# Later free times for five buffers, and three own banks for the whole of the last product

## The chip, the cores and the metric

The kernel runs on one core of a Trainium2 chip. The metric is the device time of one execution in microseconds (us). "DVE" is the vector engine, "ACT" the scalar engine, "PE" the tensor engine, "PEld" its weight loads, and "SP" the engine whose queue issues nearly all DMAs.

## The reference, cut to what matters

```python
# q, k, v: (8, 12, 448, 64); w_in: (768, 2048), w_out: (2048, 768); s, b: scalars
scores = q @ k.T / sqrt(64) - log(448)          # per batch and head
x = (sigmoid(scores) @ v)                       # regrouped to 3584 tokens x 768
h = x @ w_in
g = s * max(h, 0)**2 + b
out = g @ w_out                                 # 3584 x 768
```

## The kernel before, in words

Products in full precision are made of three reduced ones: every operand is split into a high and a low part (`PARTS`), and hi*hi, hi*lo and lo*hi are added up in PSUM. Weights arrive as 64-bit floats and are turned into 32-bit ones on chip (`convert`).

The program has three stretches. Each of the three engines and SP works in the order in which its instructions were emitted.

**Attention.** 24 steps, each with four heads of one batch (`quads`). A step ends with `store_x`: two copies from PSUM into an `xo` buffer on DVE and one DMA of 448 KB to DRAM. There are two `xo` buffers, used in turn.

**The first 512 tokens ("plain").** 16 slices of the hidden dimension, in the list `order` (0, 8, 1, 9, ...). For each slice PE makes `ffn1` (18 matmuls into a bank `ph`), ACT and DVE make the activation (relu, square, scale and bias, high part, low part: `activate`), and two slices later PE makes `ffn2` (18 matmuls). `ph` has two banks, so a slice's `ffn1` also waits for the relu of the slice two before. The weights of a slice are split by the class `Part`: high part on ACT (line 694), low part on DVE (line 638), then a store. Besides, DVE and ACT make sums of weight blocks for what comes later (`row_sums`), which nothing in this stretch needs.

**The other 3072 tokens.** Two groups of three tiles of 512 tokens. The two matrix products of each tile triple are done by a scheme with fewer products than the plain one: sums of blocks of the operands are multiplied (29 products a layer, each in two halves p = 0 and 1 of 12 matmuls of 512 columns), and results are sums of products (`sums`, `accs`). Products are chained in PSUM: a chain adds each new product onto the bank of the last one, so that the bank holds a running sum. Each of the lists `seq` has pairs (product, lane), and a lane is one PSUM tile of two banks, tagged b0 to b3. The last layer's list ends with (3, 0), (9, 1), (15, 0), (19, 1), (20, 0). The chain of lane 0 is 4, 3, 15, 20.

The order of all instructions of the last two stretches is made by a planner on the host (`Flow.run`). It has a cost for each operation, PE's order is given, and at each step it emits the operation that can start first, and of several the one due first. Where an operation needs a buffer, it can't start before the planned time at which a buffer is free (`heap.ready`). A buffer is taken from the front of a list that is sorted by that time (`Slots.tile`). The planner's time zero is the start of the plain stretch, where `ffn1` of slice 0 starts; DVE is planned from 2.0 on.

The set of buffers `cx` has 8 of its own, and from the plain stretch on 5 more, `t0` to `t4` (6 KB a partition each, in the pool `t2`). These 5 lie where the attention's buffers were: in the order in which the pools are laid out, `t0` overlaps the second `xo` buffer by 1 KB, from which the last step (the 24th) stores. At the start of the plain stretch 5 of the 8 own buffers are held: four by the tokens (`x0`), one by the weights `w1` of slice 0, which is freed by `ffn1(0)`. Two loads of weights (`convert_late`, on SP) and all weight parts of the first layer are put in `cx` as well. The second layer's parts lie in three buffers of their own, `p2`.

The very last half product (product 20, p = 1) is written differently (`last`): not onto the bank of lane 0, but in three pieces into banks of three other tags: 512 columns of the first half of the rows, and the second half in two pieces of 256 columns. The result block is then `part` (all other terms, joined on DVE with the bank of lane 0, which by then holds 4, 3, 15 and the first half of 20) plus the three pieces (`last_out`, three operations on DVE, each followed by its store).

Of the kernel before, what the change touches and what calls it, by code (L numbers as in the profile page):

```python
# [11 lines left out]
F32 = mybir.dt.float32  # L12
# [24 lines left out]
TB = 512  # L37
# [76 lines left out]
        seq=((20, 1), (23, 0), (14, 1), (27, 0), (5, 1), (18, 0), (25, 1), (13, 0), (0, 1), (17, 0),  # L114
         (15, 1), (28, 0), (3, 1), (21, 0), (19, 1), (1, 0), (24, 1), (26, 0), (22, 1), (10, 0),
         (16, 1), (11, 0), (4, 1), (7, 0), (2, 1), (9, 0), (12, 1), (8, 0), (6, 1)),
# [60 lines left out]
        seq=((0, 0), (2, 1), (1, 2), (17, 3), (27, 0), (28, 1), (21, 2), (22, 3), (18, 0), (10, 1),  # L177
         (6, 2), (13, 3), (5, 0), (26, 1), (11, 2), (12, 3), (25, 0), (23, 1), (8, 2), (16, 3),
         (4, 0), (24, 1), (7, 2), (14, 3), (3, 0), (9, 1), (15, 0), (19, 1), (20, 0)),
# [250 lines left out]
def build(net, layers, n_groups, raw_at, keep):  # L430

    flow, em = net.flow, net.em
    last = {}
    for n in range(n_groups):
        blocks = {}
        for l, L in enumerate(layers):
            seq, fresh = L["seq"], {c[0] for c in L["chains"]}
            np_ = L["np"]
            opds = {}
            count = {}  # L440
            for r, _ in seq:
                count[L["operand"][r][1:]] = count.get(L["operand"][r][1:], 0) + 1
            if l == 0:
                raw = {k: raw_at(n, k) for k in L["blocks"]}
                gets = [net.sums(raw, L["sums"], f"a{n}")] * np_
                ends = [
                    {k: (lambda v, s, k=k, p=p: blocks.__setitem__((k, p), keep(n, k, p, v, s))) for k in L["out"]}
                    for p in range(np_)
                ]
                have = [net.gather(L["accs"], ends[p], f"G{n}{p}") for p in range(np_)]  # L450
            else:
                gets = [
                    net.sums({k: blocks[em.home(k, p)] for k in L["blocks"]}, L["sums"], f"g{n}{p}")
                    for p in range(np_)
                ]
                accs = L["accs"]
                final = {k: (lambda v, s, k=k: em.out(net, n, k, v)) for k in L["out"]}
                end = n + 1 == n_groups
                if end:
                    r_last = seq[-1][0]  # L460
                    (k_last,) = (k for k, t in accs.items() if f"S{r_last}" in dict(t))
                    s_last = dict(accs[k_last])[f"S{r_last}"]
                    accs = {k: tuple(x for x in t if x[0] != f"S{r_last}") for k, t in accs.items()}
                    rest = []
                    final[k_last] = lambda v, s: rest.append((v, s))
                have = [net.gather(accs, final, f"C{n}", True)]
            for x, (r, lane) in enumerate(seq):
                row, name, sign = L["operand"][r]
                for p in range(np_):
                    key = (name, sign, p if l else 0)  # L470
                    if key not in opds:
                        v = gets[p](name)
                        opds[key] = net.split(v, sign, f"{'sg'[l]}{n}_{r}_{p}")
                        opds[key].uses = count[name, sign] * (1 if l else np_)
                    o = opds[key]
                    tag = 2 * lane + p if l == 0 else lane
                    new = r in fresh and (l == 0 or p == 0)
                    if l == 0 or p == 0:
                        bank = Bank(tag, l, None if new else last[tag])
                        waits = last[tag].readers if tag in last else []  # L480
                        last[tag] = bank
                    else:
                        bank, waits = last[tag], []
                    stop = l == 0 or p == np_ - 1
                    final_unit = l and end and x == len(seq) - 1 and p == np_ - 1
                    if final_unit:
                        part = net.join(*rest[0], Val(u, 1, bank), s_last, f"C{n}_e", True)
                        part.name = k_last
                        waits = [q for t, b in last.items() if t != tag for q in b.readers]

                    ended = None
                    seeds = r in L["seeds"] and not (l and end and x == len(seq) - 1)
                    if seeds and (l == 0 or p == 0):
                        seed = net.seeded(have[p if l == 0 else 0], f"S{r}", bank, waits, f"e{n}{l}_{r}_{p}")
                    if seeds and seed:
                        if l == 0 or p == 0:
                            waits = [seed[2]]
                        new = False
                        ended = seed

                    def fn(n=n, l=l, r=r, p=p, o=o, bank=bank, new=new, stop=stop, final_unit=final_unit):
                        if final_unit:
                            em.last(n, r, p, o, bank.tag)
                        else:
                            em.unit(n, l, r, p, o, bank, new, stop)
                        o.uses -= 1
                        if not o.uses:
                            flow.heap.free(o.hi)
                            flow.heap.free(o.lo)

                    u = em.matmuls(flow, net.UNIT, fn, [o.by, *waits], n, l, r, p)
                    if final_unit:
                        flow.op("DVE", 2.0, lambda: em.last_out(n, part, s_last), (u, part.by))
                    if stop and ended:
                        v = Val(u, 1, bank)
                        if l == 0:
                            ends[p][ended[0]](v, ended[1])
                        else:
                            final[ended[0]](net.copied(v, ended[1], f"C{n}_{ended[0]}"), 1)
                    elif stop and not final_unit:  # L520
                        have[p if l == 0 else 0](f"S{r}", Val(u, 1, bank))
# [3 lines left out]
def sigmoid_attention_relu2_ffn(  # L525
# [11 lines left out]
    B, NQ, P, _, _, S = qk.shape  # L537
    D = v.shape[5]
    NF, _, DM = w_in.shape
# [13 lines left out]
    def pool(stack, name, bufs, side=None, space=None):  # L553
        kw = dict(side=side) if side else {}
        if space is not None:
            kw["space"] = space
        return stack.enter_context(
            tc.tile_pool(name=name, bufs=bufs, reuse_waits="tile", **kw)
        )
# [37 lines left out]
    cx = Slots(cx_pool, 8, "c", spare=3)  # L597
# [24 lines left out]
    def paired(ap):  # L622
        return ap.rearrange("p (a b) -> p b a", a=2)
# [388 lines left out]
    for n, (b, t) in enumerate(quads):  # L1012
# [27 lines left out]
        last = al if n else firsts[0]  # L1040
        if n + 1 < NL:
            al = scores_last(*quads[n + 1], loaded[n + 1])
        attn_v_last(loaded[n], last, pav)
        if n and n + 1 in TWO:
            parts_lo(loaded[n + 1])
# [12 lines left out]
    rt, p2, gp = Slots(rt_pool, 2, "r"), Slots(p2_pool, 3, "w"), Slots(gp_pool, 3, "g")  # L1058
    ps_o = pool(blk_ps, "ps_o", 1, space=PSUM)
    t2 = pool(blk, "t2", 1)  # L1060
    cx.more(t2, 5, "t")
    wfp_late = pool(blk, "wfp_late", 1)
    for _, f in late:
        wf_tile(0, f, wfp_late)
# [29 lines left out]
    LAST = ((0, slice(0, TB)), (1, slice(0, TB // 2)), (1, slice(TB // 2, TB)))  # L1094

    class Emit:
# [74 lines left out]
                        )  # L1171
                        m += 1

        def last(self, n, r, p, o, busy):
            wt = fetched[stream.index((n, 1, r, p))]
            tags = [x for x in range(4) if x != busy]
            self.ends = []
            for e, tk in LAST:
                b = ps.tile([P, 2, TB], F32, tag=f"b{tags.pop(0)}", name=f"o_{e}_{tk.start}")[:, 0, tk]
                q = 0  # L1180
                for f in range(2):
                    for wi, gi in PARTS:
                        nc.tensor.matmul(
                            b, wt[:, f, wi, e * P : (e + 1) * P], paired((o.hi, o.lo)[gi][:, f, tk]),
                            start=q == 0, stop=q == 5, skip_group_check=True,
                        )
                        q += 1
                self.ends.append(b)

        def last_out(self, n, part, sign):  # L1190
            m, k = self.block[part.name]
# [51 lines left out]
    em = Emit()  # L1243
    net = Net(flow, em)
# [360 lines left out]
    plain()  # L1605
    later_sums(*LATER_SUMS)
    build(net, LAYERS, len(threes), load_raw, finish)
    flow.run({"DVE": 2.0})

# [38 lines left out]
```

## Time and profile before

| | |
|---|---|
| median of 3 runs | 977.67 us (976.95 to 978.43) |
| the profiled execution, its own time | 977.93 us |
| its span, first to last instruction | 976.1 us |
| PE busy | 970.9 us, 5192 matmuls |
| PE weight loads busy | 764.8 us |
| DVE busy | 875.8 us, 995 instructions |
| ACT busy | 719.8 us, 807 instructions |
| granted TensorE clock | 1.0 of full speed in every slice |

The span is what the profiler saw between the first and the last instruction; the device time holds 1.8 us more. A busy PE is not PE at its best, since the ends of matmuls are modelled and overlap; the distance between starts is the better measure.

### The profile page before, as it was taken

To read this page: it belongs to the slowest core of one execution; us is meant where nothing else is said; L and a number is where in the kernel's file an instruction comes from. 1 tells how busy PE (TensorE), PEld (TensorE's weight loads), DVE (VectorE), ACT (ScalarE), POOL (GpSimd) and SP (SyncE) were. 2 spreads that over 40 slices of the span, in tenths; PEclk is the share of its full clock that TensorE was granted. 3 is DMA by queue.
4 is the path that set the end of the run, shared out by engine and by line. 5 is a ranking of instruction groups with operands and counts; after the bars stand their busy time and mean duration, and the time that the engine had idled before them with its cause. 6 is when DMAs were issued, how large, how long until landed. Compare 5 with 4: busy or idle time off the path is not lost.

```text
span 976.1 us, 13892 instructions
## 1 busy us (share of the span) xinstructions
PE 970.9 (99%) x5192; PEld 764.8 (78%) x5192; DVE 875.8 (90%) x995; ACT 719.8 (74%) x807; POOL 0.2 (0%) x4
## 2 busy tenths in 40 slices
PE   9999999999999999999999999999999999999998
PEld 4555545555788888888888888888888888888887
DVE  5998999999899988899999999999787649999995
ACT  7999999999777767557799996333457499995330
POOL 0000000000000000000000000000000000000000
PEclk9999999999999999999999999999999999999999
DMA  8789999998569999989986666799866666666675
GB/s 327 286 308 350 326 364 401 351 396 311 191 263 365 354 403 413 414 279 320 341 287 206 202 203 205 226 333 330 311 201 202 207 200 207 200 205 202 201 251 194
DMA packets 97377, 276.68 MB, mean 283 GB/s; under 512 B 10016, under 2 KB 23456, under 8 KB 97312
## 3 DMA queue, kind: packets, MB, share of 16 engines
q1 hardware_dynamic: 97024, 275.35, 81.2%
q8 instruction: 41, 0.67, 0.3%
q10 hardware_dynamic: 288, 0.46, 0.1%
q14 instruction: 24, 0.20, 0.1%
HBM read 193.99 MB, written 81.79 MB: 283 GB/s over the span
## 4 chain that ended last, share of the span: by engine, by line
PE 97%; ACT 1%; DVE 1%; issue 0%; DMA 0%; DVEq 0%; ACTq 0%
PE o L1166 30%; PE h L1166 27%; PE pav L845 11%; PE psc L812 7%; PE po L1374 6%; PE ph L981 6%; PE e L1166 4%; PE psc_l L833 2%; PE pav L853 2%; PE pav L812 1%; DVE C L635 0%; ACT a L788 0%; PE idle L873 0%; DMA xd<-xo 0%; ACT w L694 0%
## 5 line engine op out<-in xcount | busy, mean ns | idle before, releaser
L1166 PE MATMUL h<-s_0h,wu 128*128 128x512 f32 x800 | 239.2, 379 | 0.0
L1166 PEld LDWEIGHTS h<-s_0h,wu 128*128 128x128 f32 x800 | 151.2, 189 | 21.5
L1166 PE MATMUL h<-s_0l,wu 128*128 128x512 f32 x400 | 151.6, 379 | 0.0
L1166 PE MATMUL o<-g_0h,wu 128*128 128x512 f32 x464 | 147.5, 379 | 0.0
L1166 PE MATMUL o<-g_1h,wu 128*128 128x512 f32 x456 | 144.9, 379 | 0.0
L788 ACT ACTIVATE a<-psc,nls 128x896 f32<-128x896 f32 x120 | 113.7, 1027 | 10.4 <-PE psc L812 8.3
L845 PE MATMUL pav<-a,v 128*64 128x448 f32 x576 | 113.8, 543 | 0.0
L1166 PEld LDWEIGHTS o<-g_0h,wu 128*128 128x128 f32 x464 | 87.7, 189 | 12.4
L1166 PEld LDWEIGHTS o<-g_1h,wu 128*128 128x128 f32 x456 | 86.2, 189 | 12.2
L845 PEld LDWEIGHTS pav<-a,v 128*64 128x64 f32 x576 | 39.1, 137 | 62.7 <-issue 56.0
L1166 PE MATMUL o<-g_0l,wu 128*128 128x512 f32 x232 | 87.9, 379 | 0.0
L1166 PE MATMUL o<-g_1l,wu 128*128 128x512 f32 x228 | 86.4, 379 | 0.0
L1166 PEld LDWEIGHTS h<-s_0l,wu 128*128 128x128 f32 x400 | 75.6, 189 | 10.7
L1258 ACT ACTIVATE G<-G 128x1024 f32<-128x1024 f32 x56 | 57.7, 1049 | 27.2 <-DVE G L638 13.6
L1374 PE MATMUL po<-g,w 128*128 128x512 f32 x288 | 64.4, 379 | 0.0
L1374 PEld LDWEIGHTS po<-g,w 128*128 128x128 f32 x288 | 54.4, 189 | 7.7
L981 PE MATMUL ph<-x0h,w 128*128 128x512 f32 x192 | 59.8, 380 | 0.3 <-ACT r L1505 0.3
L1128 ACT COPY G<-h 128x1024 f32<-128x1024 f32 x36 | 36.0, 1013 | 29.1 <-PE h L1166 28.3
L638 DVE TENSOR_TENSOR qkl<-qk,qkh 128x1664 fp32r<-128x1664 f32 (+3 forms) x26 | 44.9, 1726 | 13.9 <-ACT qkh L767 13.6
L1258 ACT ACTIVATE G<-G,b_sb,s_sb 128x1024 f32<-128x1024 f32 x40 | 49.0, 1235 | 0.1
L1166 PEld LDWEIGHTS o<-g_0l,wu 128*128 128x128 f32 x232 | 43.8, 189 | 6.2
L1166 PEld LDWEIGHTS o<-g_1l,wu 128*128 128x128 f32 x228 | 43.1, 189 | 6.1
(195 smaller groups left out, 1908.0 us busy)
## 6 DMA issues: line engine op xcount, KB each, us to landing
wu<-wd SPq DMA_DIRECT2D x232, 512.0 KB, 4.4
wd<-t SPq DMA_DIRECT2D x42, 768.0 KB, 7.5
qk<-qk_t SPq DMA_DIRECT2D x23, 896.0 KB, 7.4
st<-w_out SPq DMA_DIRECT2D x16, 768.0 KB, 8.8
st<-w_in SPq DMA_DIRECT2D x16, 768.0 KB, 9.2
v<-v_t SPq DMA_DIRECT2D x24, 448.0 KB, 5.7
xd<-xo SPq DMA_DIRECT2D x24, 448.0 KB, 4.3
out_t<-C SPq DMA_DIRECT2D x17, 512.0 KB, 5.0
```

The costliest lines, as they stand in the source:

```text
L638: nc.vector.tensor_tensor(o, x, y, op=ALU.subtract)
L788: nc.scalar.activation(a, psc[:, :, :S], AF.Sigmoid, bias=nls, scale=SCALE)
L812: nc.tensor.matmul(o[j][:, :S], two[wi][r, i, cols], paired(two[xi][r, i, :S]), start=m == 0, stop=m == 2,)
L833: nc.tensor.matmul(spread(psc[half[i], j, :S]), x[r, i, 1, 3 * P :], x[r, i, 0, :], start=True, stop=True,)
L845: nc.tensor.matmul(pav[i][r, :S], ld_[1][:, 3 * i + c, j, :], a[i, c][:, j, :], start=c == 0, stop=False,)
L853: nc.tensor.matmul(pav[i][r, :S], ld_[1][half[i], 6, j, :], a[half[i], j, :], start=False, stop=True,)
L981: nc.tensor.matmul(ph, w[:, k, wi, kc * P : (kc + 1) * P], paired(x0[h][xi][:, cc, :]), start=m == 0, stop=m == 3 * NCC - 1,)
L1128: nc.scalar.copy(o, self.view(x, l))
L1166: nc.tensor.matmul(bank.t[0][:, j], wt[:, w, wi, x * P : (x + 1) * P], paired((o.hi, o.lo)[xi][:, c, :]), start=new and m == 0, stop=stop ...
L1258: v.by = flow.op("ACT", cost, lambda: nc.scalar.activation(f32(v.t), f32(v.t), *a, **kw), (v.by,))
L1374: nc.tensor.matmul(pos[e], w[:, k, wi, kc * P : (kc + 1) * P], paired(g[:, gi, :]), start=first and i == 0, stop=last and i == 2,)
```

## The change

It has two parts. The five buffers `t0` to `t4` get a planned free time of 5.0 in place of 0.0. And both halves of the last product, not only the second, are written into the three pieces; the third piece then lies in a bank of lane 0's own tag, the first two in those of the two lanes that are no longer used. `part` takes the bank of lane 0 as it is after product 15 (`b_was`).

```diff
                     if l == 0 or p == 0:
-                        bank = Bank(tag, l, None if new else last[tag])
-                        waits = last[tag].readers if tag in last else []
+                        b_was = last.get(tag)
+                        bank = Bank(tag, l, None if new else b_was)
+                        waits = b_was.readers if b_was else []
                         last[tag] = bank
                     else:
                         bank, waits = last[tag], []
                     stop = l == 0 or p == np_ - 1
-                    final_unit = l and end and x == len(seq) - 1 and p == np_ - 1
-                    if final_unit:
-                        part = net.join(*rest[0], Val(u, 1, bank), s_last, f"C{n}_e", True)
+                    final_unit = l and end and x == len(seq) - 1
+                    if final_unit and p == 0:
+                        assert not new and seq[-2][1] != lane
+                        part = net.join(*rest[0], Val(b_was.by, 1, b_was), s_last, f"C{n}_e", True)
                         part.name = k_last
-                        waits = [q for t, b in last.items() if t != tag for q in b.readers]
+                        tags = sorted((t for t in last if t != seq[-2][1]), key=lambda t: t == tag)
+                        waits = [q for t in tags for q in (b_was if t == tag else last[t]).readers]
...
                         if final_unit:
-                            em.last(n, r, p, o, bank.tag)
+                            em.last(n, r, p, o, tags, p == 0, stop)
                         else:
                             em.unit(n, l, r, p, o, bank, new, stop)
...
                     u = em.matmuls(flow, net.UNIT, fn, [o.by, *waits], n, l, r, p)
-                    if final_unit:
+                    if final_unit and stop:
                         flow.op("DVE", 2.0, lambda: em.last_out(n, part, s_last), (u, part.by))
+                    bank.by = u
...
-    cx.more(t2, 5, "t")
+    cx.more(t2, 5, "t", lambda i: 5.0)
...
-        def last(self, n, r, p, o, busy):
+        def last(self, n, r, p, o, tags, new, stop):
             wt = fetched[stream.index((n, 1, r, p))]
-            tags = [x for x in range(4) if x != busy]
-            self.ends = []
-            for e, tk in LAST:
-                b = ps.tile([P, 2, TB], F32, tag=f"b{tags.pop(0)}", name=f"o_{e}_{tk.start}")[:, 0, tk]
+            if new:
+                self.ends = [
+                    ps.tile([P, 2, TB], F32, tag=f"b{t}", name=f"o_{e}_{tk.start}")[:, 0, tk]
+                    for t, (e, tk) in zip(tags, LAST)
+                ]
+            for (e, tk), b in zip(LAST, self.ends):
                 q = 0
                 for f in range(2):
                     for wi, gi in PARTS:
                         nc.tensor.matmul(
                             b, wt[:, f, wi, e * P : (e + 1) * P], paired((o.hi, o.lo)[gi][:, f, tk]),
-                            start=q == 0, stop=q == 5, skip_group_check=True,
+                            start=new and q == 0, stop=stop and q == 5, skip_group_check=True,
                         )
                         q += 1
-                self.ends.append(b)
```

## Rows read from the trace of the kernel before

**Rows 1.** PE's own waits, whole span (total us, times, longest).

```profile
PE idle L873 <- PEq L1638: 0.8, 1, 0.8
PE ph L981 <- ACT r L1505: 0.3, 1, 0.3
```

**Rows 2.** Waits of all engines, 236 to 260 us.

```profile
ACT w L694 <- DMA xd<-xo: 5.3, 1, 5.3
```

**Rows 3.** Chain that ended last, 232 to 260 us (start, us, what).

```profile
247.53 3.08 DMA xd<-xo
...
250.71 3.03 ACT w L694 x4
```

**Rows 4.** Timeline of PE, start of the plain stretch (start, us, what).

```profile
245.93 0.48 PE L981 MATMUL ph<-x0h,w 128*128 128x512 f32 x1
...
253.59 0.38 PE L981 MATMUL ph<-x0h,w 128*128 128x512 f32 x1
254.29 0.48 PE L981 MATMUL ph<-x0h,w 128*128 128x512 f32 x1 [0.32 <-ACT r L1505]
254.61 0.38 PE L981 MATMUL ph<-x0l,w 128*128 128x512 f32 x1
```

**Rows 5.** Timeline of ACT, same stretch.

```profile
244.49 0.88 ACT L694 CAST w<-wf 128x768 fp32r<-128x768 f32 x1
...
253.64 0.59 ACT L1505 ACTIVATE r<-ph 128x512 f32<-128x512 f32 x1
```

**Rows 6.** Timeline of DVE, same stretch.

```profile
247.42 0.95 DVE L638 TENSOR_TENSOR w<-wf,w 128x768 fp32r<-128x768 f32 x1
...
256.76 0.42 DVE L638 TENSOR_TENSOR t<-wf,wf 128x256 f32<-128x256 f32 x1
```

**Rows 7.** Busy time by stretch: PE, PEld, DVE, ACT, POOL, clock, DMA share, GB/s.

```profile
520.00:672.00 152.00, 152.00 (x706) 133.11 (x705) 151.78 (x134) 99.55 (x101) 0.00 (x0) 1.00 0.75 234
```

**Rows 8.** Timeline of PE, the last product.

```profile
966.64 0.38 PE L1166 MATMUL o<-g_0h,wu 128*128 128x512 f32 x1
...
969.23 0.38 PE L1183 MATMUL o<-g_1h,wu 128*128 128x512 f32 x1
...
970.63 0.28 PE L1183 MATMUL o<-g_1l,wu 128*128 128x256 f32 x1
...
971.75 0.28 PE L1183 MATMUL o<-g_1h,wu 128*128 128x256 f32 x1
```

**Rows 9.** Timeline of DVE, the last products.

```profile
962.86 1.21 DVE L638 TENSOR_TENSOR C<-C,o 128x1024 f32<-128x1024 f32 x1
966.84 1.22 DVE L635 TENSOR_TENSOR C_t<-C_t,o 128x1024 f32<-128x1024 f32 x1 [2.77 <-PE o L1166]
...
970.37 1.21 DVE L635 TENSOR_TENSOR C<-C,o 128x1024 f32<-128x1024 f32 x1
```

**Rows 10.** Chain that ended last, 960 to 977 us.

```profile
971.69 0.69 DVE C L635
...
972.71 0.33 DVE C L635
```

**Rows 11.** Timeline of SP's queue, the last stores.

```profile
972.41 0.34 SPq L1204 DMA_DIRECT2D out_t<-C  x1
...
973.32 0.46 SPq L1204 DMA_DIRECT2D out_t<-C  x1
```

**Rows 12.** Busy time by stretch, the tail; columns as in rows 7.

```profile
970.30:972.90 2.60, 1.73 (x14) 1.50 (x12) 2.50 (x5) 0.00 (x0) 0.00 (x0) 1.00 1.02 398
972.90:973.30 0.40, 0.00 (x0) 0.00 (x0) 0.14 (x1) 0.00 (x0) 0.00 (x0) 1.00 0.11 41
973.30:974.00 0.70, 0.00 (x0) 0.00 (x0) 0.00 (x0) 0.00 (x0) 0.00 (x0) 1.00 1.00 372
974.00:974.80 0.80, 0.00 (x0) 0.00 (x0) 0.00 (x0) 0.00 (x0) 0.00 (x0) 1.00 1.05 311
```

## The prediction, made before the change was run

> **What bounds the kernel now.** I read PE's own waits first, since a kernel that multiplies nearly all the time can only gain where PE stands still or before and after it. In the whole span PE waits twice [rows 1]: 0.8 us at the start of the program, which the change doesn't touch, and 0.3 us for the relu of the plain stretch. From 254.29 to the last matmul at 971.75 it has no wait at all. So everything that the two edits can save lies in two places: around 254 us, and behind the last product, between 972 us and the end of the span at 976.1.
>
> For the first place I read the waits of all engines there, then the chain. ACT stood still for 5.3 us, until the store of the attention's last output had landed [rows 2]. That store was issued at 247.53, took 3.08 us, and four weight splits followed [rows 3]. The relu of slice 0 stood behind them in ACT's queue and ran only at 253.64 [rows 5], though `ffn1(0)` had ended long before: 18 matmuls of 0.216 us (the distance of the twelve between 966.64 and 969.23 in [rows 8] is 2.59 us) from 245.93 [rows 4] end at about 250.0. PE went on with slice 8, and only the third `ffn1`, which needs the bank that the late relu reads, had to wait.
>
> For the second place I read the timelines of PE, DVE and SP and the rate of DMA. PE is done at 971.75 + 0.28 = 972.03 [rows 8]. DVE isn't: at 970.37 it makes the join `part` [rows 9], and the operations on the three pieces run from 971.69 to 972.71 + 0.33 = 973.04 [rows 10]. The first piece was ready on PE at about 969.23 + 6 x 0.216 + 0.16 = 970.69, so it waited a full microsecond for DVE.
>
> **The change part by part.**
>
> *The free time of 5.0.* What PE loses in the first place: after the matmul at 253.59 the next would have started at 253.81, it started at 254.29, which is 0.48; and from it to the following one it took 0.32 in place of 0.216, another 0.10 [rows 4]. Sum 0.59 us (rounded up in the last digit). The 5.3 us of ACT and what DVE lost behind them cost nothing more, because PE never waits again.
>
> Which instruction writes `t0`, the buffer over the stored one? In the plan of before, three own buffers are free at 0.0; the split of slice 8 and the two loads take them, and the next split, of slice 1, takes `t0` at once. That is the ACT instruction at 250.71. With the change the list is: `w1`'s buffer, free at 3.89 by the planned cost of `ffn1(0)`, then the five at 5.0. Slice 1's split then takes `w1`'s buffer at 3.89, and the planner puts the split of the second layer's slice 0, which lies in `p2`, ahead of it. On the chip ACT then runs: the split at 244.49 [rows 5], the second layer's split to about 246.2, then a wait for `ffn1(0)` to about 250.05, slice 1's split (0.83) to 250.9, the relu (0.59) to 251.5. The wait of ACT isn't gone, it becomes one of about 3.8 us for PE, but behind it the relu stands second and not fifth. What is late next: the third `ffn1` is due at 253.81 and needs this relu (251.5) and the low part of slice 1 on DVE (0.95 us after 250.95, so 251.9). Cover of 1.9 us; if it were gone, the third `ffn1` would again wait, with the 0.59 as the price for the first half microsecond and one for one beyond. The first user of `t0` is now planned at 5.0 or later, which is 245.93 + 5.0 = 250.93 on the chip, and the store landed at 250.61: it waits little or not at all. The weight sums of DVE, which started at 256.76 [rows 6], start some 4 us earlier. No instruction, byte or DMA is added. Gain: 0.59, bounds 0 (the stall stays in another form) and 0.59 (PE can't have more than it lost).
>
> The planner orders everything from there on anew, since its choices feed on each other. In the profile PE has no wait behind 254.61, so nothing can be gained there, and what can be lost is not shown by any row. I take nothing, and keep a loss for the rivals.
>
> *The last product.* PE: the half p = 0 has 12 matmuls of 0.216 = 2.59 us. Its new form has 6 of 512 columns and 12 of 256. Ten distances of the latter take 971.75 - 970.63 = 1.12 us [rows 8], so 0.112 each. 6 x 0.216 + 12 x 0.112 = 2.64: PE ends 0.05 later, at 972.08. The Trainium skill (TensorE: Matmul & The Clock Gate, section "Back-to-back issue gap") gives lower sustained distances, 131 ns at 512 columns and 81 at 128; an estimate between the two for 256 is 98 ns, and by these the new form would cost 0.39 us more than the old, most of what the tail can bring. The trace has 216 and 112 instead, so I don't count with it.
>
> DVE: the join `part` no longer needs p = 0. It needs product 15, which DVE reads for two other joins, the second at 962.86 [rows 9]; after them DVE stands idle for 2.77 us until 966.84. The join of 1.2 us fits there whole. If it goes first of the three, the other two and their stores move back by 1.14 us, still inside that gap. PE's third piece, which takes over the bank that the join reads, starts at 966.64 + 1.30 + 0.67 = 968.6, three microseconds after the join.
>
> At the end DVE is then free where the join starts now, at about 970.4, and takes the pieces as PE delivers them: the first at 970.8, the second at 971.45, the third at 971.75 + 0.05 + 0.28 + 0.04 = 972.12. The small operation takes 0.41 (two of them end the kernel, 972.71 + 0.33 being the end of the second): 972.53 in place of 973.04, a gain of 0.51. SP issues the last store now 0.28 after DVE's end, at 973.32 [rows 11], because three issues follow each other; with the first two out earlier it goes at 972.56, a gain of 0.76.
>
> But the bytes have to go out too. The two 512 KB stores ahead fill the engines from 970.3 to 972.9 at 398 GB/s; there is a hole of 0.4 us, and then the last three (512 KB in all) take until about 974.75 [rows 12]. Issue to first byte is 0.9 us (972.41 to 973.3). With the issues some 0.8 us earlier the hole closes and no more: the last bytes are out 0.4 earlier. So the tail's bounds are 0.4 (the transfers decide) and 0.76 (the last issue decides). I take 0.45, near the lower end, since the rows show the engines full on both sides of the hole.
>
> *Sum.* 0.59 + 0.45 = 1.04 us. The profiled execution's 977.93 becomes 976.89, its span 975.06. That execution was 0.26 above the median of the runs, 977.67, so the median becomes 976.6.
>
> **The rivals.**
>
> *The first gain doesn't come.* ACT has a new wait of 3.8 us; if DVE's first sum lands on `t0` ahead of slice 1's low part and the store is late, or the split of slice 1 goes behind more work than I count, the third `ffn1` waits as before. For it: the store took 3.08 us in a quiet queue and has a margin of 0.3. Against it: 1.9 us of cover. Time 977.67 - 0.45 = 977.2.
>
> *The second gain turns.* If `part` is emitted behind the operation at 966.84, which waits for PE, it runs from 968.1 to 969.3, and PE, whose third piece may begin at 968.6, waits for it by 0.7. The end moves from 973.04 to about 972.12 + 0.7 + 0.41 = 973.2, 0.2 later than now. Against it: `part` is due with PE's unit, the others only with stores. It decides once the join starts later than 967.4. Time 977.67 - 0.59 + 0.2 = 977.3.
>
> *Slower: the new order makes DVE a bound.* In 520 to 672 DVE is busy for 151.78 of 152 us [rows 7], and PE's second layer reads low parts that DVE makes. Each full-size operation there takes 1.14 us a piece in sequence. If the anew ordered queue puts one more of them ahead of a low part than PE's lead allows, PE waits 1.14 for each. One eats the gain: 977.7. To be slower than before by what can be told it takes three; with four the time is 976.6 + 4.6 = 981.2. For it: no slack in DVE's total. Against it: in the whole stretch PE waited for nothing, and DVE gets about 4 us of work done earlier.
>
> *More than forecast.* PE would have to gain elsewhere, and it waits nowhere else; only a tail ruled by the last issue (976.3) is open.
>
> **How the numbers follow.** Forecast 0.66 (976.1 to 977.0), first gain missing 0.12, second turned 0.07, one or two new stalls of 1.14 (977.7 to 978.9) 0.06, three or more 0.06, something better than 975.7 by a cause that I don't see 0.03. About 0.2%, 1.95 us, is what a measurement of this kernel can tell from no change; the limits are 975.7 and 979.6. So faster 0.03, same 0.91, slower 0.06. The range of 975.8 to 977.8 holds the forecast, the first two rivals, a single stall, and the scatter of the runs before (0.7 to each side).
>
> **What would show it.** PE's waits: the one on the relu is gone, and the first matmul of the third `ffn1` starts 7.9 us after the first of `ffn1(0)`, not 8.36. ACT: no wait on `xd<-xo` of more than some tenths, one of about 3.8 us on `ph`. DVE at the end: the full-size join with `o` between 961.7 and 966, in before's times, and the three small operations right after PE's pieces. Tail: no hole in the DMA rate between the two big stores and the last three. Wrong I would be by any new wait of PE behind 254 us, or by a tail of the old length behind the last matmul (4.1 us; I expect 3.6).

## The result, and the profile after

The change makes the kernel slower: 988.01 us (median of 4 runs, 987.44 to 989.93) against 977.87 (4 runs, 976.95 to 978.43), a ratio of 1.0104 [1.0092, 1.0117]. I had forecast 976.6, with a range of 975.8 to 977.8. Of the first experiment's eleven executions one, at 1128.25 us, was in a slow state and is left out of its median and ratio. The profiled execution took 987.44 us; its span is 985.6 where it was 976.1. The 9.5 us between the two spans divide as follows, by the pieces of the chains that ended last in both traces.

| stretch | before | after | difference | forecast |
|---|---|---|---|---|
| start to PE's first matmul of the plain stretch | 245.93 | 245.62 | -0.31 | 0 |
| from there to the first product of the first layer | 125.17 | 126.45 | +1.28 | -0.59 |
| from there to the first product of the second layer (first group) | 150.22 | 159.22 | +9.00 | 0 |
| from there to PE's end | 450.71 | 450.76 | +0.05 | +0.05 |
| behind PE's end | 4.1 | 3.6 | -0.5 | -0.50 |

The first row is scatter: over the ten traces of this case that start lies between 245.29 and 246.56. The chains' pieces for the third row, of before and then of after (start, us, what):

```profile
371.10 113.96 PE h L1166 x528
...
521.32 150.22 PE o L1166 x696
```

```profile
372.07 49.22 PE h L1170 x228
...
531.29 150.22 PE o L1170 x696
```

PE's own waits, as for the kernel before in [rows 1]: engine and line, what it waited for, us in total, times, longest.

```profile
PE h L1170 <- DVE s_0l L642: 6.6, 2, 5.5
PE ph L985 <- DVE w L642: 0.9, 1, 0.9
PE idle L877 <- PEq L1643: 0.8, 1, 0.8
PE po L1379 <- DVE g L642: 0.5, 1, 0.5
...
```

The wait for the relu is gone. In its place stand two in the plain stretch (`ph`, `po`) and 6.6 us in the first layer, for the low parts of two products' operands (`s_0l`).

**The plain stretch.** First ACT's timeline at its start (start, us, what; in brackets the idle time before it and what ended it). Its line of 431 belongs to the first layer, below.

```profile
249.81 0.83 ACT L698 CAST w<-wf 128x768 fp32r<-128x768 f32 x1 [3.14 <-PE ph L985]
250.54 0.59 ACT L1510 ACTIVATE r<-ph 128x512 f32<-128x512 f32 x1
...
431.08 1.03 ACT L1149 CAST s_0h<-a 128x1024 fp32r<-128x1024 f32 x1
```

ACT does what I had worked out: no wait for the store, one for PE instead (3.14 us, where I had 3.8), and the relu at 250.54, not 253.64 [rows 5]. Then PE's timeline, with the first layer and the last matmul below:

```profile
253.27 0.59 PE L985 MATMUL ph<-x0h,w 128*128 128x512 f32 x2
253.71 0.38 PE L985 MATMUL ph<-x0l,w 128*128 128x512 f32 x1
254.97 0.70 PE L985 MATMUL ph<-x0h,w 128*128 128x512 f32 x2 [0.88 <-DVE w L642]
...
450.34 0.79 PE L1170 MATMUL h<-s_0l,wu 128*128 128x512 f32 x1 [5.54 <-DVE s_0l L642]
...
451.78 0.63 PE L1170 MATMUL h<-s_0l,wu 128*128 128x512 f32 x1
452.21 1.06 PE L1170 MATMUL h<-s_0h,wu 128*128 128x512 f32 x2
...
457.02 0.59 PE L1170 MATMUL h<-s_0h,wu 128*128 128x512 f32 x2
458.72 0.48 PE L1170 MATMUL h<-s_0l,wu 128*128 128x512 f32 x1 [1.10 <-DVE s_0l L642]
...
981.77 0.28 PE L1189 MATMUL o<-g_1h,wu 128*128 128x256 f32 x1
```

The third `ffn1` starts on time: the second of the two matmuls at 253.27, at about 253.49, is its first, 7.87 us behind that of `ffn1(0)`. Its third matmul is the first that reads the low part of slice 1's weights. It was due at 253.92 and came at 254.97. DVE's timeline says why:

```profile
247.10 1.82 DVE L642 TENSOR_TENSOR w<-wf,w 128x768 fp32r<-128x768 f32 x2
253.32 0.73 DVE L663 TENSOR_SCALAR wf<-st 128x768 int32<-128x768 int32 x1 [4.39 <-DMA st<-w_in]
253.97 0.94 DVE L642 TENSOR_TENSOR w<-wf,w 128x768 fp32r<-128x768 f32 x1
...
258.62 0.68 DVE L642 TENSOR_TENSOR g<-r,g 128x512 fp32r<-128x512 f32 x1
...
449.06 1.23 DVE L642 TENSOR_TENSOR s_0l<-a,s_0h 128x1024 fp32r<-128x1024 f32 x1 [1.28 <-DMA wd<-t_t]
...
971.69 1.22 DVE L639 TENSOR_TENSOR C<-C,o 128x1024 f32<-128x1024 f32 x1 [4.01 <-PE o L1170]
...
980.74 1.09 DVE L639 TENSOR_TENSOR C<-C,o 128x512 f32<-128x512 f32 x2 [0.31 <-PE o L1189]
982.08 0.42 DVE L639 TENSOR_TENSOR C<-C,o 128x256 f32<-128x256 f32 x1 [0.25 <-PE o L1189]
```

The low part of slice 1 (253.97) stands behind an operation that converts late weights (line 663), and that one waits 4.39 us for its load. The high part that it needs was there at 250.64 (249.81 + 0.83), so it is DVE's order that holds it back, and not ACT's new wait. SP's timeline has the load's issue:

```profile
247.22 0.32 SPq L866 DMA_DIRECT2D xd<-xo  x1
247.63 1.67 SPq L1405 DMA_DIRECT2D st<-w_in  x2
```

SP issued it only behind the attention's last store, 2.0 us after PE's start. What DVE has behind comes late too, the low part of `g` (258.62) among it, for which PE stands still once more.

**The first layer.** The chain that ended last, around the long wait (start, us, what):

```profile
438.18 4.92 DMA wd<-t_t
...
443.18 1.01 ACT G L1132
444.19 1.14 ACT G_t L1263
445.33 0.78 ACT G L1132
446.11 2.86 DMA wd<-t_t
...
449.06 1.24 DVE s_0l L642
...
450.34 7.08 PE h L1170 x23
...
457.44 1.24 DVE s_0l L642
```

The high part of this operand (product 19, p = 0) is there from 431.08 + 1.03 on. The low part takes 1.23 us and needs nothing but the high part, its source and a buffer. It is made at 449.06, 17 us later. Until 447.8 DVE makes other operations, which the new order puts ahead of it, and stands idle at times; in the last 1.28 us it waits until a store of weight sums (`wd<-t_t`) has landed and its buffer is free. In the trace of before the high part ran at 430.71 and the low part at 437.35; the third line is the low part of the next product, 1:

```profile
430.71 1.03 ACT L1145 CAST s_0h<-a 128x1024 fp32r<-128x1024 f32 x1
437.35 1.22 DVE L638 TENSOR_TENSOR s_0l<-a,s_0h 128x1024 fp32r<-128x1024 f32 x1
...
444.96 1.23 DVE L638 TENSOR_TENSOR s_0l<-a,s_0h 128x1024 fp32r<-128x1024 f32 x1 [0.61 <-DMA wd<-t_t]
```

Busy time by stretch shows the rest (columns as in rows 7):

```profile
444.00:450.30 6.30, 0.81 (x4) 0.38 (x2) 4.78 (x5) 6.24 (x8) 0.00 (x0) 0.76 0.78 281
450.30:451.30 1.00, 0.96 (x2) 0.83 (x3) 0.87 (x2) 0.96 (x2) 0.00 (x0) 0.50 0.00 0
...
453.30:454.30 1.00, 1.00 (x4) 0.79 (x4) 0.00 (x0) 0.00 (x0) 0.00 (x0) 0.61 1.02 414
454.30:455.30 1.00, 1.00 (x7) 0.87 (x5) 0.45 (x1) 0.00 (x0) 0.00 (x0) 1.00 0.88 356
...
980.60:981.40 0.80, 0.80 (x9) 0.80 (x8) 0.66 (x1) 0.00 (x0) 0.00 (x0) 1.00 1.05 410
981.40:982.20 0.80, 0.64 (x6) 0.45 (x5) 0.55 (x3) 0.00 (x0) 0.00 (x0) 1.00 1.06 410
982.20:983.00 0.80, 0.00 (x0) 0.00 (x0) 0.30 (x1) 0.00 (x0) 0.00 (x0) 1.00 1.05 405
```

When PE goes on at 450.34 its granted clock is 0.50 of full speed, 1.2 GHz, until about 454. From there to the start of the 23rd matmul, at 457.02, pass 6.68 us, where 22 distances of 0.216 are 4.75. So the 9.00 us are 5.54 + 1.10 = 6.64 of waits, 1.93 of longer distances at the lower clock, and some 0.43 at the two restarts. Of these, twice 0.16 arise because a matmul that had to wait doesn't start before the (modelled) end of the one ahead of it, and 0.10 in the first distance behind the second wait.

**The tail** went as forecast. DVE makes the join of `part` in the row of three that begins at 971.69, where it made two [rows 9]; it then takes the pieces as PE delivers them; and the rate of DMA stays between 405 and 410 GB/s where it had its hole [rows 12]. From PE's end at 982.05 to the end of the span it takes 3.6 us.

### The profile page after: what moved, and what is told of

It is laid out like the page before. It is cut to its first block, busy times and chain, and to the rows that moved or that the text cites. A ratio compares the mean times of both kernels' runs of the same rounds, so it can differ in the third digit from the quotient of the medians.

```text
span 985.6 us, 13920 instructions
## 1 busy us (share of the span) xinstructions
PE 973.1 (99%) x5198; PEld 765.9 (78%) x5198; DVE 878.0 (89%) x995; ACT 720.4 (73%) x807; POOL 0.2 (0%) x4
## 4 chain that ended last, share of the span: by engine, by line
PE 94%; DVE 2%; DMA 2%; ACT 1%; issue 1%; SPq 0%; ACTq 0%; DVEq 0%
PE o L1170 30%; PE h L1170 24%; PE pav L849 11%; PE psc L816 7%; PE po L1379 6%; PE ph L985 5%; PE e L1170 4%; PE psc_l L837 2%; PE pav L857 2%; PE pav L816 1%; DMA wd<-t_t 1%; DMA st<-w_in 1%; DVE G L639 1%; PE o L1189 1%; DVE s_0l L642 0%
## 5 line engine op out<-in xcount | busy, mean ns | idle before, releaser
L1170 PE MATMUL o<-g_0h,wu 128*128 128x512 f32 x456 | 144.9, 379 | 0.0
```

Source lines behind the costliest of these rows:

```text
L1170: nc.tensor.matmul(bank.t[0][:, j], wt[:, w, wi, x * P : (x + 1) * P], paired((o.hi, o.lo)[xi][:, c, :]), start=new and m == 0, stop=stop ...
```

## The experiments

**Which of the two parts costs?** Theory A: the free times, by the order that the planner makes of them. Theory B: the new last product. Each part alone:

```diff
  # tail only: the changed kernel with
-    cx.more(t2, 5, "t", lambda i: 5.0)
+    cx.more(t2, 5, "t")
  # five only: the kernel before with
-    cx.more(t2, 5, "t")
+    cx.more(t2, 5, "t", lambda i: 5.0)
```

> The changed kernel with the five buffers free at 0.0 again; only the new last product is left. Theory A (the loss of 10 us comes from the order that the planner writes with 5.0): faster than before by the tail alone, 0.45 to 0.55 us, so about 977.4; PE has its 0.3 us wait for the relu at 254 as before and no wait behind it. Theory B (the new last product, whose waits enter the planner's due times, makes the loss): slower than before by about 9 us, with the 5.5 us wait of PE for a low part near 445. Theory C (the weight sums' stores land later on the chip than planned, in whatever order): as A or between, with waits of PE in 430 to 470.

Measured: 977.70 us, ratio 0.9996 [0.9986, 1.0005]: by its time alone the new last product can't be told from none. In the trace ACT's wait for the store is there again (5.50 us), PE waits for nothing behind 255 us, and the tail takes 3.6 us, 0.5 less than before.

> The kernel before with only the free time of 5.0 for all five buffers. Theory A: about 10.5 us slower than before, 988.5: PE waits about 5.5 and 1.1 us for two low parts near 445 to 458, runs at the lower clock for some us behind the first wait, loses 1.9 us against the ideal at the start of the plain stretch, and the tail is the old one (4.1 us behind the last matmul). Theory B: as before within 0.3 us. Theory C: as A.

Measured: 989.89 us, 1.0117 [1.0103, 1.0131], with a tail of 4.1 us; it is 1.4 above what I expected, and the long wait is 6.5 us and not 5.5. PE's waits in it:

```profile
PE h L1166 <- DVE s_0l L638: 7.6, 2, 6.5
...
PE ph L981 <- DVE w L638: 0.6, 1, 0.6
PE po L1374 <- DVE g L638: 0.6, 1, 0.6
```

The whole loss belongs to the free times; B fell. So did C, since the first run has no wait of PE between 430 and 470. The last product alone moves the tail and nothing else.

**Is it enough to hold back the one buffer that overlaps?**

```diff
-    cx.more(t2, 5, "t", lambda i: 5.0)
+    cx.more(t2, 5, "t", lambda i: 0.0 if i else 5.0)
```

> The changed kernel with 5.0 for the one buffer that lies over the stored output (t0) and 0.0 for the other four. Theory A: the order of all engines is that of before except in the last product, so no new wait of PE; ACT's wait of 5.3 us and PE's 0.3 us wait at 254 go (0.59 us), the tail gives 0.5: 1.0 to 1.1 us faster than before, about 976.8. Theory C (a late store stalls this stretch however it is ordered) or a rival in which the stall at 254 moves to another buffer: only the tail's 0.5, 977.4.

Measured: 977.75 us, 0.9997 [0.9988, 1.0006]. The first layer is without a wait, but the stall at 254 us is as it was. ACT's timeline:

```profile
250.61 3.03 ACT L698 CAST w<-wf 128x768 fp32r<-128x768 f32 x4 [5.57 <-DMA xd<-xo]
```

The addresses in the built program say why: the five places of the pool are given out in the order of first use, not of name. With `t0` held back `t1` is used first, and gets the lowest place, the one over the stored output. What was written of `t0` ahead of the prediction holds for whichever of the five comes first.

**What is in the plan itself?** The planner can be run by itself, and its times can be read beside the trace. By its own times PE never stands still within the first layer before the change; after it PE has a gap of 5.32 us ahead of product 19 and one of 1.34 ahead of product 1. Their sum is 6.66; the trace has 6.64. The lines of the plan around the low part (planned start, when due, engine, what; last the number of free buffers after it):

```
before
  190.67 due 195.5  DVE  weight sum t5                4
  ...
  191.29 due 197.3  DVE  low part of product 19       4
after
  191.56 due 195.5  DVE  weight sum t5                2
  192.18 due 200.4  DVE  join for product 1           4
  192.59 due 199.9  ACT  copy of a product            3
  193.32 due 196.2  DVE  weight sum t6                2
  193.54 due 201.3  ACT  high part of product 1       1
  ...
  200.16 due 292.2  ACT  (other work)                 1
  201.47 due 197.3  DVE  low part of product 19       1
```

After the change the next buffer that the low part may have is planned free at 192.29. DVE is free at 192.18. The planner takes what can start first, and that is a join due three microseconds later than the low part. By the time the join is done, copies and high parts on ACT have the buffers, and the list stays nearly empty until 201.47. The difference of 0.11 us is what tips it. If the loss comes from such an accident of the order, and not from late free times as such, it should go away for other free times. Of the plans for free times from 0.5 to 10, those for 4.9, 5.0, 5.1, 5.5 and 6 have the gap, those up to 4.5 and from 7 on have none. One was run from either side:

```diff
-    cx.more(t2, 5, "t", lambda i: 5.0)
+    cx.more(t2, 5, "t", lambda i: 4.5)     # and, in another run, 7.0
```

> The changed kernel with 4.5 in place of 5.0 for all five buffers. A half microsecond in the planner; on the chip no transfer changes. Theory A: the order of the later stretch is another one, in which the low part of product 19 is made before the buffers run out; PE has no wait near 445, and the time is 0.5 to 1.1 us below before, 976.8 to 977.4. Theory C, or a theory in which late free times as such do the harm: about 10 us slower than before, as with 5.0.

Measured: 979.69 us, 1.0016 [1.0007, 1.0025]. No wait is left near 445 us, as expected, but the time is higher than I said. PE's waits in it:

```profile
PE po L1379 <- DVE g L642: 1.6, 1, 1.6
...
PE h L1170 <- DVE s_0l L642: 0.6, 1, 0.6
```

The plain stretch takes 126.43 us, 1.26 more than before. DVE waits there, in turn, 1.32 us for the store and 1.25 and 1.64 us for the two loads, since 4.5 is earlier than the store lands and the plan has the loads too early. The first layer takes 1.04 us longer than before, nearly all of it at one wait of 0.58 us, at 383.05, for a low part that stands behind four sums on DVE. The plan of this version has no gap there: a plan without gaps doesn't promise a run without waits.

> The changed kernel with 7.0 in place of 5.0. Theory A: the order at the start keeps the converted weight slice ahead of slice 1's low part on DVE, as with 5.0, so PE loses 1.3 to 1.9 us there; but product 19's low part is made in time, and no wait near 445 is left: 978.5 to 979.5. A theory in which a later free time does more harm: above 988.

Measured: 979.85 us, 1.0018 [1.0009, 1.0027], slightly above what I expected. The first layer takes 150.22 us again, to the last digit that of before. The plain stretch takes 127.47 (+2.30): DVE waits 5.06 us for the late weights' load, and PE 1.38 and 0.97 us behind it.

**Is it this low part?** The changed kernel, with one rule lifted for this operation alone: it counts as needing no buffer when the planner looks for its earliest start, so it doesn't wait for a buffer's planned free time. Its due time stays, and it still takes a buffer. In the plan it then stands at 192.18, not at 201.47.

```diff
-        o.by = self.flow.op("DVE", self.ADD, lo, (a,), lambda: 1)
+        o.by = self.flow.op("DVE", self.ADD, lo, (a,), lambda: int(name != "s0_19_0"))
```

> The changed kernel (5.0 for all five) with one planner rule lifted for one operation: the low part of product 19's operand in the first group may be planned without waiting for a buffer's free time. All else follows from the same rules; 46 of some 1,900 operations stand elsewhere. Theory A (in that stretch the buffers run out, and this low part gets its one late): the 5.5 us wait of PE before product 19 goes, smaller waits stay a little later since the buffers are still short, in all 2 to 4 us, and the time is 4 to 7 us below the changed kernel's, about 982 to 984. If the 9 us have another cause than this one operation's buffer, the time stays at 988.

Measured: 982.24 us, 1.0043 [1.0029, 1.0056]. Of the 9.00 us in the first layer 3.05 are left, and PE's waits there are short:

```profile
PE h L1170 <- DVE s_0l L1157: 1.5, 1, 1.5
PE h L1170 <- DVE s_0l L642: 1.0, 1, 1.0
```

The granted clock is 1.00 from 440 to 462. So the rule on the buffer, for one operation, makes two thirds of the 9.00 us. With this operation 46 of some 1,900 stand elsewhere in the plan. The other third are waits for the low parts of the next two products, 1 and 24; that they come from the same want of buffers is argued, and no run tried it with more buffers.

**Can the gain at 254 us be had without it?** Two ways. The first takes the wait away by moving memory: the pool of the late converted weights is laid out ahead of the five buffers, so that it lies over the stored output, and the free times stay 0. The last line of the edit tells the planner of the new places.

```diff
+    wfp_late = pool(blk, "wfp_late", 1)
+    for _, f in late:
+        wf_tile(0, f, wfp_late)
     t2 = pool(blk, "t2", 1)
-    cx.more(t2, 5, "t", lambda i: 5.0)
-    wfp_late = pool(blk, "wfp_late", 1)
-    for _, f in late:
-        wf_tile(0, f, wfp_late)
+    cx.more(t2, 5, "t")
...
-            left += gp.left(gp_pool, 4096) + cx.left(t2, 6144) + [(2 * 3072, read)]
+            left += gp.left(gp_pool, 4096) + [(2 * 3072, read)] + cx.left(t2, 6144)
```

> The new last product, all five buffers free at 0.0 as before, but the pool of two late weight tiles laid ahead of the five buffers, so that none of them lies over the stored output, whichever is used first; the order of every engine is that of run e1. Theory A': the wait of ACT for the store depends on the place of the buffer used first, so it goes here and only here; the relu runs at about 250 and PE doesn't wait for it. What is late next is the low part of the first activation, which stands on DVE behind the second converted weight slice (landed at 256.1 before): PE's first second-layer product may wait some 0.1 to 0.2 us. Gain at the start 0.4 to 0.6, tail 0.45: 0.85 to 1.05 us below before, 977.1 or so. Rival: the wait moves to another buffer as in e3, and only the tail's 0.4 is left.

Measured: 977.23 us, 0.9988 [0.9979, 0.9997]. ACT's timeline, to be read against [rows 2, 5]:

```profile
246.25 3.03 ACT L698 CAST w<-wf 128x768 fp32r<-128x768 f32 x4 [0.72 <-PE pav L857]
250.28 0.60 ACT L1510 ACTIVATE r<-ph 128x512 f32<-128x512 f32 x1 [1.00 <-PE ph L985]
```

The four splits no longer wait for the store and the relu follows its `ffn1` at once. PE waits nowhere behind the start of the plain stretch, which takes 124.68 us, 0.49 less than before.

The second way keeps the change and tells the planner the truth on the loads as well: SP, like DVE, is planned from 2.0 on.

```diff
-    flow.run({"DVE": 2.0})
+    flow.run({"DVE": 2.0, "SP": 2.0})
```

> The changed kernel (5.0 for all five) with SP planned from 2.0 on, since its first load of the plain stretch goes out about 2.0 us after the first product there (247.63 against 245.62 in the changed kernel), behind the last store. Theory A'': the loss at the start is that of a DVE operation planned for a load that is thought to land 2 us earlier than it does; with 2.0 the low parts stand ahead of it, PE has no wait at 254 to 260, no wait near 445, and the tail is the new one: 1.0 us below before, 976.9 to 977.2. If the start's loss comes from ACT's new wait for PE instead, PE still waits at 254 and the time is 978 to 979.

Measured: 976.98 us, 0.9987 [0.9978, 0.9995]. DVE's timeline at the start:

```profile
247.46 4.52 DVE L642 TENSOR_TENSOR w<-wf,w 128x768 fp32r<-128x768 f32 x5
...
254.98 0.68 DVE L663 TENSOR_SCALAR wf<-st 128x768 int32<-128x768 int32 x1 [2.65 <-DMA st<-w_in]
```

The five low parts now stand ahead of the operation that waits for the load, and PE waits for nothing behind it. The plan is another one in more than this: the loads no longer take own buffers at 0.0, so slice 1's split is made early, ahead of ACT's wait for PE, and the plan has no gap at products 19 and 1. PE has no wait at all after the program's start, the plain stretch takes 124.59 us (-0.58), the first layer 150.22. Both versions beat the kernel before by 1.1 to 1.4 us against its runs beside them (978.36; the intervals of the two ratios reach from 0.3 to 2.2 us), which is about the 1.04 us that I had forecast for the change.

## Why the prediction was wrong

**The step that failed** is the paragraph "The planner orders everything from there on anew ... I take nothing". I argued from PE's waits in the trace of before that nothing could be gained, which holds, and left the price of a new order at zero because no row shows it. The price was 9.00 us, two thirds of it in one operation. A list of PE's waits shows how long PE waits, and not how near it came to waiting: before the change the list of free buffers ran low at the same place, and the low part still got one in time. Rows for this were in the trace of before, but not among PE's waits. The low parts of products 19 and 1 ended at 438.57 and 446.19, and PE first read them at 443.68 and 448.86: 5.1 and 2.7 us of slack. The second of them, and some high parts on ACT, had already waited for a store to free a buffer. The planner's own times would have shown the gap before any run.

**The cover of 1.9 us** for the third `ffn1` was the second wrong step. I followed ACT's queue operation by operation, rightly to within 0.7 us, and took from DVE's queue only the one that I needed: the low part of slice 1, ready by 251.9. It was ready at 254.9. The plan has the load at time 0 and its data at 4.47, so it puts the conversion ahead of the low part; on the chip SP is not free before 2.0. The term that I set at -0.59 became +1.28. e8, where this order is mended, has -0.58: the size of the gain was right, and so was the stall's cause (e5, where the buffers are moved and the order kept, has -0.49), but the kernel as changed doesn't reach it.

**The last product** was right: part early, no wait of PE for it, PE 0.05 us later, the tail 0.5 shorter (0.45 net, forecast 0.45). The lower end, where the transfers decide, was the right one to take. The distances of 0.216 and 0.112 us held.

**The rivals.** "The first gain doesn't come" is true as far as it goes. "Slower: the new order makes DVE a bound" has the right sign and the right kind of waiter, PE for low parts, with 0.06; its place and its mechanism were wrong. I looked where DVE is busy throughout (520 to 672), and priced a stall by DVE's operations of 1.14 us. It came where DVE has idle time, waiting itself for buffers, at 5.54 and 1.10 us, and the clock added 1.93. The scarce thing was buffers, not an engine.

What stays open: the price of the lower clock was read from the spacing of the matmuls and not tried apart from the waits, and why the plain stretch in the run with 7.0 loses somewhat more than I expected was not followed up.

## What to carry to other kernels

Where a list scheduler orders a kernel, a planned time is no local edit: run the plan before and after, and compare its own gaps on the engine that bounds, and how many buffers are free where they come. A wait that comes from two things lying at one address is better removed by moving one of them, which leaves the plan alone; and if a time is corrected in the plan, the others that are wrong by as much (here the loads' issue) have to be corrected with it. Gaps in the plan are a warning, but a plan without them is no proof (the wait at 383 with 4.5). When a trace shows no waits of the bounding engine, that doesn't say how much slack there is: read it from the timelines, as the time between an operand's end and its first use.

## What the runs showed of the hardware

The clock made a stall dearer than itself. PE stood still for 5.54 us, went on at a granted clock of 0.50 until about 454, and lost 1.93 us more by it. With the part of the free times alone it was the same: a wait of 6.51 us, then 0.50 from 452 to 454. Behind waits of 1.5 and 1.0 us, in the run with the rule lifted for one low part, the clock stayed at 1.00, as it did behind the second wait of the changed kernel (1.10). The Trainium skill (TensorE: Matmul & The Clock Gate, section "Wait — 56ns, not 53.3ns?") gives 426.7 ns from start to start at 512 columns at the lower clock and 215.7 at the higher; the trace agrees, with 0.43 us between 451.78 and 452.21 and 0.216 elsewhere.
